# Rebuilding 32-bit weights from 64-bit words: a scaled copy on ScalarE in place of a mask, and three VectorE instructions per piece in another order

## The chip, the cores and the metric

The kernel runs on one core of a Trainium2 chip. The metric is the device time of one execution in microseconds (us), as the median of several runs. The engines of the core work from queues of their own, each strictly in order: PE (TensorE) multiplies matrices, DVE (VectorE) and ACT (ScalarE) do elementwise work, POOL (GpSimd) has only a little to do at the start, and SP (SyncE) issues most of the DMAs. An instruction waits for others through semaphores; whatever stands behind a waiting instruction in its queue waits too.

## The reference

```python
def _attn_ref(x, w_r, w_i, b_r, b_i):            # x: (2, 3008, 256)
    X = np.fft.rfft(x, axis=1)
    Yr = Xr @ w_r - Xi @ w_i + b_r
    Yi = Xr @ w_i + Xi @ w_r + b_i
    Yr = np.sign(Yr) * np.maximum(np.abs(Yr) - 0.01, 0.0)   # Yi the same
    return np.fft.irfft(Yr + 1j * Yi, n=3008, axis=1)

def _moe_ref(x, w_in, w_out):                     # d_ff 2048, on 6016 tokens
    h = x @ w_in
    return (h * np.clip(h + 3.0, 0.0, 6.0) / 6.0) @ w_out

def _moe2_ref(x, w_gate, w_val, w_out):           # d_ff 1536
    g = x @ w_gate
    return ((g / (1.0 + np.exp(-g))) * (x @ w_val)) @ w_out
```

The five weight matrices of the two dense layers come as 64-bit floats; everything is computed in 32 bits.

## The kernel before, in words

**Stages.** A Fourier stage comes first: `pre` (first transform, L242 on PE, with copies `bs` on ACT at L245 and DVE at L247), `s2` (second transform, L284, whose result is split into a high part `xh` by ACT at L288 and L289 and a low part `xl` by DVE at L118), `ln` (24 small products, L113 to L115 with tile `p`, then `yb`, `yc`, `yp` on DVE at L319 to L323), `ia` and `post` (back transforms, L330 and L416). Each product is three matmuls, low times high, high times low and high times high, so every operand needs both parts. The first dense layer follows as 192 *units* of a block of up to 512 tokens and one of 16 column groups (`project1`, tile `ph`; `lower`, tiles `gh` and `gl`; `outp`, tile `acc`), and begins while the second half of the Fourier stage still runs. The second dense layer comes last (`quad`, from L652 on).

**Order.** Nothing is reordered: each queue has its instructions in the order in which the program writes them. The list `seq` sets it for the Fourier stage: for each step, `ln` half 0, `ia`, a `pre`, the two halves of `s2` for the next step, `ln` half 1, a `pre` while there are any, `ia`. Within `s2` the second half's `xh` stands on ACT behind a negated copy (L291) of the first half's `xl`, so DVE and ACT take turns there.

**The weights.** The class `Convert` turns the 64-bit weights into 32-bit ones, piece by piece (128 partitions of 256 numbers): 32 pieces for the first dense layer (`conv1`) and 36 for the second (`conv2`). A DMA on SP brings a piece into tile `st` (four buffers). Of each number the upper word H has the sign, 11 bits of exponent and 20 of mantissa, the lower word L the other 32. A 32-bit float is put together from them by shifts and masks on DVE, in tile `wt`: L164 takes H three bits to the left and masks it, L165 puts the top three bits of L below, L166 the two top bits of H above, and L172 multiplies by zero where the number is too small, by comparing a mask `mask` that ACT made by squaring H (L156). Each of L165, L166 and L172 reads what the instruction just ahead of it wrote. For `conv1`, ACT then makes the high part (L175, `w1h`) two steps later, and DVE the low part (L179, `w1l`) three steps later. `step` runs the stages of different pieces one after the other. Its calls stand at fixed places: in `ln`, in the later `pre` and, twice at most, in each of the first units, so `conv1` is done shortly after the Fourier stage. `conv2` runs beside the units, one step for two units, and its results go back to HBM (`Wd`), to be fetched for the second dense layer.

Of the kernel before, what the change touches and what calls it, by code (L numbers as in the profile page):

```python
# [9 lines left out]
F32 = mybir.dt.float32  # L10
F32R = mybir.dt.float32r
I64 = mybir.dt.int64
U32 = mybir.dt.uint32
AF = mybir.ActivationFunctionType
ALU = mybir.AluOpType
# [10 lines left out]
NQ = NG // 4  # L26
LAM = 0.01

LEAST = 1.125 * 2.0**-15
FF1, FF2 = 2048, 1536  # L30
KF1, KF2 = FF1 // 128, FF2 // 128
BLK = 512
# [45 lines left out]
def fourier_moe_kernel(ctx: ExitStack, tc: tile.TileContext, x, lin, bias, w1, w2, fwd1, inv2, fwd2,  # L78
                       inv1, out):
    nc = tc.nc  # L80

    def pool(stack, name, side):
        return stack.enter_context(tc.tile_pool(name=name, bufs=1, side=side))
# [33 lines left out]
    def low(o, full, hi):  # L117
        nc.vector.tensor_tensor(out=o, in0=full, in1=hi.bitcast(F32), op=ALU.subtract)  # L118
# [11 lines left out]
    wst = pool(ctx, "wst", "left")  # L130
# [6 lines left out]
    class Convert:  # L137
# [2 lines left out]

        def __init__(self, pieces):
            self.pieces = pieces
            self.st, self.mask, self.full = {}, {}, {}
            self.at = -3

        def done(self):
# [4 lines left out]
            nc.sync.dma_start(t, self.pieces[i][0])  # L151
            self.st[i] = t.bitcast(U32).rearrange("p (n t) -> p n t", t=2)

        def square(self, i):
            m = wst.tile([128, 256], F32, tag="mask", name="mask", bufs=2)
            nc.scalar.activation(m, self.st[i][:, :, 1].bitcast(F32), AF.Square)  # L156
            self.mask[i] = m

        def words(self, i, to=None):
            st, m = self.st.pop(i), self.mask.pop(i)  # L160
            H, L = st[:, :, 1], st[:, :, 0]
            t = wst.tile([128, 256], U32, tag="wt", name="wt", bufs=4)
            v = nc.vector
            v.tensor_scalar(t, H, 3, 0x3FFFFFF8, op0=ALU.logical_shift_left, op1=ALU.bitwise_and)  # L164
            v.scalar_tensor_tensor(out=t, in0=L, scalar=29, in1=t, op0=ALU.logical_shift_right, op1=ALU.bitwise_or)  # L165
            v.scalar_tensor_tensor(out=t, in0=H, scalar=0xC0000000, in1=t, op0=ALU.bitwise_and, op1=ALU.bitwise_or)  # L166
            tf = t.bitcast(F32)
            if to is None:
                to = self.full[i] = tf
            else:  # L170
                m, tf = (a.rearrange("p (a b) -> p a b", b=128) for a in (m, tf))
            v.scalar_tensor_tensor(out=to, in0=m, scalar=LEAST * LEAST, in1=tf, op0=ALU.is_ge, op1=ALU.mult)  # L172

        def high(self, i):
            nc.scalar.copy(self.pieces[i][1], self.full[i])  # L175
# [5 lines left out]
        def step(self):  # L181
            i = self.at
            self.at += 1
            for at, stage in ((i - 3, self.low), (i - 2, self.high), (i + 1, self.square), (i, self.words), (i + 3, self.load)):
                if 0 <= at < len(self.pieces):
                    stage(at)

# [32 lines left out]
    p = psf[0]([128, 512], "p0")  # L220
# [130 lines left out]
    def L(p):  # L351
        return [lambda h=h: ln(*ORDER[p], h) for h in range(2)]

    def A(p):
        return [lambda h=h: ia(*ORDER[p], h) for h in range(2)] if p >= 0 else [lambda: None] * 2
# [9 lines left out]
    for p in range(len(ORDER)):  # L365
        l, a = L(p), A(p - 1)
# [101 lines left out]
    for k, after in zip(blocks, blocks[1:]):  # L468
        for f, step in ((2, lambda k=after: load_ct(k)), (7, lambda k=after: post(k, 0)),
                        (9, lambda k=after: post(k, 1))):  # L470
            extra.setdefault((k, f), []).append(step)

    at = [0]
    more = []

    def unit():

        n = at[0]
        at[0] += 1

        for _ in range(2):
            if conv1.at < 2 * n + 6 and not conv1.done():
                conv1.step()
        if 0 <= n - 1 < len(units):
            lower(units[n - 1])
        if n < len(units):
            k, f = units[n]
            state[units[n]] = project1(k, f, ntok(k))
        if n >= 2:
            outp(units[n - 2])  # L490
        if n < len(units):
            for step in extra.get(units[n], ()):
                step()
        for f in more:
            f(n)
# [16 lines left out]
    def ring():  # L512
        return cv.tile([128, SLOT, 128], F32R, tag="slot", name="slot", bufs=4)

    class Convert2(Convert):
# [8 lines left out]
            return full[f, 2]  # L524

        def steps(self):
            for i in range(3):
                self.load(i)
            self.square(0)
            yield  # L530
            for f in range(KF2):
                for what in range(3):
                    i = 3 * f + what
                    if i + 3 < len(self.pieces):
                        self.load(i + 3)
                    if i + 1 < len(self.pieces):
                        self.square(i + 1)
                    self.words(i, self.full_of(i))
                    yield
                F = full.pop(f)  # L540
                for o, x, y, op in ((4, 0, 3, ALU.add), (5, 4, 1, ALU.subtract), (6, 1, 0, ALU.subtract), (7, 2, 5, ALU.subtract)):
                    nc.vector.tensor_tensor(out=F[:, o], in0=F[:, x], in1=F[:, y], op=op)
                t = ring()
                nc.scalar.copy(t[:, :7], F[:, 1:])
                yield
                O = full.pop((f, 2))
                nc.scalar.copy(t[:, 14:16], O)
                low(t[:, 7:14], F[:, 1:], t[:, :7])
                yield
                low(t[:, 16:], O, t[:, 14:16])  # L550
                nc.sync.dma_start(Wd[f], t.bitcast(F32).rearrange("p a b -> p (a b)"))
                yield
# [59 lines left out]
    def beside(n):  # L612
        if not conv1.done():
            conv1.step()
        elif n % 2 == 0:
            next(steps, None)
        left = len(units) + 2 - n
        if left <= 28:
            next(first, lambda: None)()
        if left in (8, 4):  # L620
            fetch(2 - left // 4)

    more.append(beside)
    while at[0] < len(units) + 2:
        unit()
    assert next(steps, True) and next(first, None) is None


# [170 lines left out]
```

## Time and profile before

| | us |
|---|---|
| median of 3 runs | 1257.1 |
| lowest, highest | 1257.02, 1259.64 |
| span of the profiled execution, first to last instruction | 1255.8 |
| PE busy | 1233.0 |
| DVE busy | 845.7 |
| ACT busy | 679.5 |

The profile is of one execution. A busy time is the time in which an engine's instructions ran; a PE that is busy may still run at half its clock, so the granted clock has to be read with it. What an engine waits for is given as the releaser, the instruction whose semaphore came last. Of each instruction the timeline has the start and the duration; on DVE and ACT an instruction can start a little before the end of the one ahead.

### The profile page before, as it was taken

The numbers are of one execution on the slowest core, as the hardware profiler recorded it, in microseconds if no ns is written. First come the engines' busy times: TensorE is split into PE (matmuls) and PEld (weight loads), VectorE is DVE, ScalarE is ACT, GpSimd is POOL, SyncE is SP. The second block draws the span as 40 slices with busy tenths as digits, with TensorE's granted clock in tenths as the row PEclk, the third lists the DMA queues.
The fourth block names the chain that finished last, engine by engine and source line by source line (L and its number), as shares of the span: only waits on it lengthen the run. The fifth ranks groups of instructions, "written<-read, shape, count | busy, mean of one in ns | idle before, by whom it ended". The sixth has DMA issues, their size and how long they took to land.

```text
span 1255.8 us, 15966 instructions
## 1 busy us (share of the span) xinstructions
PE 1233.0 (98%) x5914; PEld 1035.6 (82%) x5914; DVE 845.7 (67%) x1492; ACT 679.5 (54%) x1216; POOL 6.3 (0%) x15
## 2 busy tenths in 40 slices
PE   8889999999999999999999999999999999999998
PEld 2789898788888888888889878888888888888997
DVE  2588767676666676676666567677676676666665
ACT  2344445455555555555555465566556665555554
POOL 1000000000000000000000000000000000000000
PEclk9899999999999999999999999999999999999999
DMA  9965511231321221232132054554544644544551
GB/s 300 277 220 160 169 42 64 93 99 63 97 95 55 90 89 49 93 99 83 54 104 91 25 212 151 201 187 169 203 166 156 229 171 153 214 153 164 207 184 72
DMA packets 50286, 172.85 MB, mean 138 GB/s; under 512 B 4752, under 2 KB 18160, under 8 KB 39456
## 3 DMA queue, kind: packets, MB, share of 16 engines
q1 hardware_dynamic: 41856, 158.55, 36.7%
q10 hardware_dynamic: 8128, 12.58, 2.9%
q8 instruction: 46, 0.75, 0.2%
q0 software_dynamic: 224, 0.69, 0.2%
q14 instruction: 32, 0.26, 0.1%
HBM read 132.75 MB, written 39.06 MB: 137 GB/s over the span
## 4 chain that ended last, share of the span: by engine, by line
PE 90%; DVE 5%; DMA 2%; ACT 2%; issue 1%; ACTq 0%; DVEq 0%; SPq 0%
PE acc L114 12%; PE acc L115 12%; PE acc L113 12%; PE ph L113 7%; PE ph L115 7%; PE ph L114 7%; PE P L652 5%; PE P L654 5%; PE P L653 5%; PE p L416 3%; PE Tb L652 3%; PE Tb L653 3%; PE Tb L654 3%; PE Q L652 1%; PE Q L654 1%; PE Q L653 1%
## 5 line engine op out<-in xcount | busy, mean ns | idle before, releaser
L118 DVE TENSOR_TENSOR gl<-r,gh 128x512 fp32r<-128x512 f32 (+1 forms) x192 | 130.1, 677 | 79.8 <-ACT gh L449 78.6
L430 ACT ACTIVATE r<-ph,three 128x512 f32<-128x512 f32 (+1 forms) x192 | 130.2, 678 | 96.5 <-PE ph L115 78.3
L431 DVE SCALAR_TENSOR_TENSOR r<-r,ph 128x512 f32<-128x512 f32 (+1 forms) x192 | 129.4, 674 | 61.1 <-ACT r L430 60.4
L449 ACT CAST gh<-r 128x512 fp32r<-128x512 f32 (+1 forms) x192 | 117.4, 611 | 87.5 <-DVE r L431 86.6
L113 PE MATMUL ph<-xah,w1l 128*128 128x512 f32 (+1 forms) x384 | 152.2, 396 | 0.7 <-DVE w1l L179 0.7
L113 PE MATMUL acc<-gh,w1l 128*128 128x512 f32 (+1 forms) x384 | 148.3, 386 | 1.0 <-ACT gh L449 1.0
L114 PE MATMUL acc<-gl,w1h 128*128 128x512 f32 (+1 forms) x384 | 148.3, 386 | 0.6 <-DVE gl L118 0.5
L115 PE MATMUL ph<-xah,w1h 128*128 128x512 f32 (+1 forms) x384 | 148.2, 386 | 0.0
L114 PE MATMUL ph<-xal,w1h 128*128 128x512 f32 (+1 forms) x384 | 148.2, 386 | 0.0
L115 PE MATMUL acc<-gh,w1h 128*128 128x512 f32 (+1 forms) x384 | 148.1, 386 | 0.0
L118 DVE TENSOR_TENSOR gl<-s,gh 128x512 fp32r<-128x512 f32 (+1 forms) x144 | 97.2, 675 | 49.5 <-ACT gh L676 49.5
L652 PE MATMUL P<-xo,slot 128*128 128x512 f32 (+1 forms) x288 | 111.3, 386 | 1.7 <-DVE g L722 0.8
L114 PE MATMUL acc<-gl,slot 128*128 128x512 f32 (+1 forms) x288 | 111.1, 386 | 0.3 <-DVE gl L118 0.2
L113 PE MATMUL acc<-gh,slot 128*128 128x512 f32 (+1 forms) x288 | 111.0, 385 | 0.0
L654 PE MATMUL P<-xo,slot 128*128 128x512 f32 (+1 forms) x288 | 110.9, 385 | 0.0
L653 PE MATMUL P<-xo,slot 128*128 128x512 f32 (+1 forms) x288 | 110.9, 385 | 0.0
L115 PE MATMUL acc<-gh,slot 128*128 128x512 f32 (+1 forms) x288 | 110.9, 385 | 0.0
L718 ACT ACTIVATE s<-g 128x512 f32<-128x512 f32 (+1 forms) x72 | 44.9, 623 | 93.2 <-DVE g L716 93.2
L676 ACT CAST gh<-s 128x512 fp32r<-128x512 f32 (+1 forms) x144 | 88.1, 612 | 1.8 <-DVE s L735 1.6
L114 PEld LDWEIGHTS acc<-gl,w1h 128*128 128x128 f32 x384 | 72.1, 188 | 15.3 <-DVE gl L118 1.7
L113 PEld LDWEIGHTS acc<-gh,w1l 128*128 128x128 f32 x384 | 72.1, 188 | 15.1 <-ACT gh L449 1.5
L113 PEld LDWEIGHTS ph<-xah,w1l 128*128 128x128 f32 x384 | 72.2, 188 | 14.2 <-issue 0.8
(95 smaller groups left out, 2292.9 us busy)
## 6 DMA issues: line engine op xcount, KB each, us to landing
slot<-Wd SPq DMA_DIRECT2D x72, 1152.0 KB, 5.0
st<-in_w SPq DMA_DIRECT2D x68, 256.0 KB, 3.2
Wd<-slot SPq DMA_DIRECT2D x12, 1152.0 KB, 4.7
x<-in_x SPq DMA_DIRECT2D x16, 384.0 KB, 6.2
Bd<-bs ACTq DMA_DIRECT2D x16, 384.0 KB, 5.1
z<-Bd SPq DMA_DIRECT2D x12, 512.0 KB, 5.5
Cd<-cs ACTq DMA_DIRECT2D x12, 512.0 KB, 3.3
Xd<-x SPq DMA_DIRECT2D x20, 256.0 KB, 2.1
```

Of the source, the lines that this page charges most:

```text
L113: nc.tensor.matmul(o, wl, xh, start=start, stop=False)
L114: nc.tensor.matmul(o, wh, xl, start=False, stop=False)
L115: nc.tensor.matmul(o, wh, xh, start=False, stop=stop)
L118: nc.vector.tensor_tensor(out=o, in0=full, in1=hi.bitcast(F32), op=ALU.subtract)
L430: nc.scalar.activation(r[:, :n], p[:, :n], AF.Relu, bias=three)
L431: nc.vector.scalar_tensor_tensor(out=r[:, :n], in0=r[:, :n], scalar=6.0, in1=p[:, :n], op0=ALU.min, op1=ALU.mult)
L449: nc.scalar.copy(hi[:, :n], g[:, :n])
L652: nc.tensor.matmul(o, wl, x[:, 0, :n], start=start, stop=False, skip_group_check=not start)
L653: nc.tensor.matmul(o, wh, x[:, 1, :n], start=False, stop=False, skip_group_check=not start)
L654: nc.tensor.matmul(o, wh, x[:, 0, :n], start=False, stop=True, skip_group_check=not start)
L676: nc.scalar.copy(hi[:, :nb], t[:, :nb])
L718: nc.scalar.activation(s0[:, :n], h, AF.Silu)
```

## The change

ACT no longer squares H. It copies it, read as a 32-bit float and multiplied by 2**-112 (`scale`, tile `head`, three buffers). Read so, H has the upper eight of the eleven exponent bits as its exponent, and the factor subtracts 112 from them: that is the difference of the two formats' exponent offsets, and numbers that are too small become zero by it. DVE then has three instructions per piece where it had four: `shift` (L161 of the new file) takes `head` three bits to the left, `tail` (L165) puts in the top bits of L, and `sign` (L174) the sign bit of `head`. In a step they are those of two pieces: `shift` of piece i, `sign` of piece i - 1, `tail` of piece i. `sign`, the last of a piece, is thus a step later than L172 was; `high` and `low` keep their steps. In `conv2` the load of a piece and the ACT copy are issued behind the DVE instructions of a step instead of ahead of them, and there is one step more.

```diff
+HEAD = 2.0**-112
...
-        def square(self, i):
-            m = wst.tile([128, 256], F32, tag="mask", name="mask", bufs=2)
-            nc.scalar.activation(m, self.st[i][:, :, 1].bitcast(F32), AF.Square)
-            self.mask[i] = m
-
-        def words(self, i, to=None):
-            st, m = self.st.pop(i), self.mask.pop(i)
-            H, L = st[:, :, 1], st[:, :, 0]
-            t = wst.tile([128, 256], U32, tag="wt", name="wt", bufs=4)
-            v = nc.vector
-            v.tensor_scalar(t, H, 3, 0x3FFFFFF8, op0=ALU.logical_shift_left, op1=ALU.bitwise_and)
-            v.scalar_tensor_tensor(out=t, in0=L, scalar=29, in1=t, op0=ALU.logical_shift_right, op1=ALU.bitwise_or)
-            v.scalar_tensor_tensor(out=t, in0=H, scalar=0xC0000000, in1=t, op0=ALU.bitwise_and, op1=ALU.bitwise_or)
-            tf = t.bitcast(F32)
...
-            v.scalar_tensor_tensor(out=to, in0=m, scalar=LEAST * LEAST, in1=tf, op0=ALU.is_ge, op1=ALU.mult)
+        def scale(self, i):
+            m = wst.tile([128, 256], F32, tag="head", name="head", bufs=3)
+            nc.scalar.mul(m, self.st[i][:, :, 1].bitcast(F32), HEAD)
+            self.head[i] = m.bitcast(U32)
+
+        def shift(self, i):
+            self.word[i] = wst.tile([128, 256], U32, tag="wt", name="wt", bufs=4)
+            nc.vector.tensor_scalar(self.word[i], self.head[i], 3, None, op0=ALU.logical_shift_left)
+
+        def tail(self, i):
+            t, L = self.word[i], self.st.pop(i)[:, :, 0]
+            nc.vector.scalar_tensor_tensor(out=t, in0=L, scalar=29, in1=t, op0=ALU.logical_shift_right, op1=ALU.bitwise_or)
+
+        def sign(self, i, to=None):
+            h, t = self.head.pop(i), self.word.pop(i)
...
+            nc.vector.scalar_tensor_tensor(out=to, in0=h, scalar=0x80000000, in1=t, op0=ALU.bitwise_and, op1=ALU.bitwise_or)
...
-            for at, stage in ((i - 3, self.low), (i - 2, self.high), (i + 1, self.square), (i, self.words), (i + 3, self.load)):
+            for at, stage in ((i - 3, self.low), (i - 2, self.high), (i, self.shift), (i - 1, self.sign), (i, self.tail),
+                              (i + 1, self.scale), (i + 3, self.load)):
...
-            for f in range(KF2):
-                for what in range(3):
-                    i = 3 * f + what
-                    if i + 3 < len(self.pieces):
-                        self.load(i + 3)
-                    if i + 1 < len(self.pieces):
-                        self.square(i + 1)
-                    self.words(i, self.full_of(i))
-                    yield
+            for i in range(n + 1):
+                if i < n:
+                    self.shift(i)
+                if i > 0:
+                    self.sign(i - 1, self.full_of(i - 1))
+                if i < n:
+                    self.tail(i)
+                if i + 3 < n:
+                    self.load(i + 3)
+                if i + 1 < n:
+                    self.scale(i + 1)
+                yield
+                f, what = divmod(i - 1, 3)
+                if f < 0 or what < 2:
+                    continue
```

DVE's queue in the Fourier stage, from the last `bs` copy to the two low parts `xl` of the fourth `s2` step, before (a name in brackets is an engine's semaphore or that of a DMA queue):

```order
L247 COPY bs_7_650<-p_1_7_1_654 96x512 [waits DMAHW2_49,PE_49]
L179 TENSOR_TENSOR w1l_123<-wt,w1h_122 128x256 [waits Activation_49]
L164 TENSOR_SCALAR wt<-st 128x256 [waits DMAHW0_49]
L165 SCALAR_TENSOR_TENSOR wt<-st,wt 128x256 [waits DVE_49]
L166 SCALAR_TENSOR_TENSOR wt<-st,wt 128x256 [waits DVE_49]
L172 SCALAR_TENSOR_TENSOR wt<-mask,wt 128x256 [waits DVE_49,Activation_49]
L118 TENSOR_TENSOR xl_3_675<-p_0_3_0_676,xh_3_674 128x4x128 [waits PE_49,Activation_49]
L118 TENSOR_TENSOR xl_3_675<-p_0_3_1_685,xh_3_674 128x4x128 [waits PE_49,Activation_49]
```

The same place of DVE's queue now (all lines behind the new code are two or three higher):

```order
L250 COPY bs_7_641<-p_1_7_1_645 96x512 [waits DMAHW2_49,PE_49]
L181 TENSOR_TENSOR w1l_123<-wt,w1h_122 128x256 [waits Activation_49]
L161 TENSOR_SCALAR wt<-head 128x256 [waits Activation_49]
L174 SCALAR_TENSOR_TENSOR wt<-head,wt 128x256
L165 SCALAR_TENSOR_TENSOR wt<-st,wt 128x256 [waits DMAHW0_49,DVE_49]
L118 TENSOR_TENSOR xl_3_665<-p_0_3_0_666,xh_3_664 128x4x128 [waits PE_49,Activation_49]
L118 TENSOR_TENSOR xl_3_665<-p_0_3_1_675,xh_3_664 128x4x128 [waits PE_49,Activation_49]
```

One instruction is gone, and the wait for ACT has moved from the last instruction of a piece to its first, L161; of the other two, L174 works on the piece before.

ACT's queue where two steps of `conv1` stand in one unit, near the end of the Fourier stage, before:

```order
L175 CAST w1h_142<-wt 128x256
L156 ACTIVATE mask<-st 128x256 [waits DMAHW6_49]
L175 CAST w1h_142<-wt 128x256
L156 ACTIVATE mask<-st 128x256 [waits DMAHW0_49,DVE_49]
L449 CAST gh<-r 128x512
L430 ACTIVATE r<-ph,three 128x512 [waits PE_49]
```

ACT's queue at that place now:

```order
L177 CAST w1h_142<-wt 128x256
L156 ACTIVATE head<-st 128x256 [waits DMAHW6_49]
L177 CAST w1h_142<-wt 128x256 [waits DVE_49]
L156 ACTIVATE head<-st 128x256 [waits DMAHW0_49]
L452 CAST gh<-r 128x512
L433 ACTIVATE r<-ph,three 128x512 [waits PE_49]
```

The instructions are as many and stand in the same order; the wait for DVE went from the second L156 (for a buffer of `mask`) to the high part just ahead of it (for the `sign` of its piece).

## Rows read from the trace of the kernel before

**Rows 1.** The page's first part: busy us, share of the span, instructions of each engine

```profile
PE 1233.0 (98%) x5914; PEld 1035.6 (82%) x5914; DVE 845.7 (67%) x1492; ACT 679.5 (54%) x1216; POOL 6.3 (0%) x15
```

**Rows 2.** Stretches: length, busy PE, PEld, DVE, ACT, POOL; granted clock; DMA share; GB/s

```profile
38.40:74.28 35.88, 35.00 (x228) 29.10 (x228) 28.09 (x62) 15.67 (x39) 0.00 (x0) 1.00 0.83 261
...
79.28:82.80 3.52, 3.52 (x17) 3.52 (x18) 3.35 (x8) 2.25 (x6) 0.00 (x0) 0.52 0.40 88
...
92.46:101.81 9.35, 9.35 (x74) 9.10 (x73) 7.73 (x18) 4.71 (x12) 0.00 (x0) 1.00 0.56 192
...
111.81:121.82 10.01, 9.62 (x74) 9.16 (x73) 8.36 (x19) 4.93 (x13) 0.00 (x0) 1.00 0.49 160
121.82:128.66 6.84, 6.40 (x50) 5.86 (x48) 5.32 (x12) 2.81 (x7) 0.00 (x0) 1.00 0.79 225
184.00:209.56 25.56, 24.59 (x137) 20.73 (x135) 24.15 (x56) 12.62 (x28) 0.00 (x0) 1.00 0.17 52
...
250.00:700.00 450.00, 450.00 (x2126) 381.83 (x2125) 303.70 (x558) 244.36 (x409) 0.00 (x0) 1.00 0.24 81
```

**Rows 3.** PE's waits from 40 to 212 us: in total, times, longest

```profile
PE p L113 <- DVE xl L118: 5.2, 5, 2.7
```

**Rows 4.** PE's timeline, 60 to 80 us: start, duration, instruction, count, idle before and releaser

```profile
66.38 1.03 PE L330 MATMUL p<-yp,n 128*128 128x256 f32 x4
67.25 1.88 PE L242 MATMUL p<-x,fwd_sb 96*96 96x512 f32 x4
...
71.11 0.28 PE L113 MATMUL p<-linh,xl 128*128 128x256 f32 x1
...
71.47 0.28 PE L113 MATMUL p<-linh,xl 128*128 128x256 f32 x1
...
73.63 1.03 PE L330 MATMUL p<-yp,n 128*128 128x256 f32 x4
...
77.35 0.39 PE L113 MATMUL p<-linh,xl 128*128 128x256 f32 x1 [2.69 <-DVE xl L118]
...
79.28 0.51 PE L113 MATMUL p<-linh,xl 128*128 128x256 f32 x1 [0.86 <-DVE xl L118]
```

**Rows 5.** PE's timeline, 198 to 210 us: first and last of three waits

```profile
199.24 0.47 PE L113 MATMUL ph<-xah,w1l 128*128 128x512 f32 x1 [0.41 <-DVE w1l L179]
...
209.56 0.50 PE L113 MATMUL ph<-xah,w1l 128*128 128x512 f32 x1 [0.26 <-DVE w1l L179]
```

**Rows 6.** DVE's timeline, 70 to 77 us: one piece, and what follows up to `xl`

```profile
70.51 0.28 DVE L164 TENSOR_SCALAR wt<-st 128x256 uint32<-128x256 uint32 x1
70.83 0.43 DVE L165 SCALAR_TENSOR_TENSOR wt<-st,wt 128x256 uint32<-128x256 uint32 x1
71.29 0.42 DVE L166 SCALAR_TENSOR_TENSOR wt<-st,wt 128x256 uint32<-128x256 uint32 x1
71.82 0.42 DVE L172 SCALAR_TENSOR_TENSOR wt<-mask,wt 128x256 f32<-128x256 f32 x1
72.16 0.68 DVE L319 TENSOR_TENSOR yb<-p,bias_sb 128x512 f32<-128x512 f32 x1
...
73.95 0.68 DVE L247 COPY bs<-p 96x512 f32<-96x512 f32 x1
...
76.60 0.69 DVE L118 TENSOR_TENSOR xl<-p,xh 128x512 fp32r<-128x512 f32 x1
```

**Rows 7.** ACT's timeline, 74 to 77 us, between that `bs` and that `xl`

```profile
74.72 0.31 ACTq L249 DMA_DIRECT2D Bd<-bs  x1
...
75.38 0.43 ACT L156 ACTIVATE mask<-st 128x256 f32<-128x256 f32 x1
```

**Rows 8.** The instructions on tile `wt`: duration min/median/max in ns, first and last start

```profile
L172 DVE SCALAR_TENSOR_TENSOR wo<-mask,wt x12: 425/426/427, 243.7 to 627.6; 128x256 f32<-128x256 f32 x12
```

**Rows 9.** ACT's timeline: the first piece of `conv2`

```profile
226.74 0.43 ACT L156 ACTIVATE mask<-st 128x256 f32<-128x256 f32 x1 [4.46 <-DMA st<-in_w]
```

**Rows 10.** ACT's waits from 180 to 215 us: in total, times, longest

```profile
ACT cs L331 <- PE p L330: 3.6, 3, 1.8
```

More of the change, by code (lines that the diff above doesn't have):

```diff
@@ L27 @@
 LAM = 0.01
-LEAST = 1.125 * 2.0**-15
+HEAD = 2.0**-112
 FF1, FF2 = 2048, 1536
@@ L142, in __init__ @@
             self.pieces = pieces
-            self.st, self.mask, self.full = {}, {}, {}
+            self.st, self.head, self.word, self.full = {}, {}, {}, {}
             self.at = -3
@@ L152, in load @@
             self.st[i] = t.bitcast(U32).rearrange("p (n t) -> p n t", t=2)
-        def square(self, i):
-            m = wst.tile([128, 256], F32, tag="mask", name="mask", bufs=2)
-            nc.scalar.activation(m, self.st[i][:, :, 1].bitcast(F32), AF.Square)
-            self.mask[i] = m
-        def words(self, i, to=None):
-            st, m = self.st.pop(i), self.mask.pop(i)
-            H, L = st[:, :, 1], st[:, :, 0]
-            t = wst.tile([128, 256], U32, tag="wt", name="wt", bufs=4)
-            v = nc.vector
-            v.tensor_scalar(t, H, 3, 0x3FFFFFF8, op0=ALU.logical_shift_left, op1=ALU.bitwise_and)
-            v.scalar_tensor_tensor(out=t, in0=L, scalar=29, in1=t, op0=ALU.logical_shift_right, op1=ALU.bitwise_or)
-            v.scalar_tensor_tensor(out=t, in0=H, scalar=0xC0000000, in1=t, op0=ALU.bitwise_and, op1=ALU.bitwise_or)
-            tf = t.bitcast(F32)
+        def scale(self, i):
[10 more added lines that the diff above has]
+            h, t = self.head.pop(i), self.word.pop(i)
             if to is None:
-                to = self.full[i] = tf
+                to, self.full[i] = t, t.bitcast(F32)
             else:
-                m, tf = (a.rearrange("p (a b) -> p a b", b=128) for a in (m, tf))
-            v.scalar_tensor_tensor(out=to, in0=m, scalar=LEAST * LEAST, in1=tf, op0=ALU.is_ge, op1=ALU.mult)
+                h, t = (a.rearrange("p (a b) -> p a b", b=128) for a in (h, t))
+                to = to.bitcast(U32)
+            nc.vector.scalar_tensor_tensor(out=to, in0=h, scalar=0x80000000, in1=t, op0=ALU.bitwise_and, op1=ALU.bitwise_or)
         def high(self, i):
@@ L526, in steps @@
         def steps(self):
+            n = len(self.pieces)
             for i in range(3):
                 self.load(i)
-            self.square(0)
+            self.scale(0)
             yield
-            for f in range(KF2):
-                for what in range(3):
-                    i = 3 * f + what
-                    if i + 3 < len(self.pieces):
-                        self.load(i + 3)
-                    if i + 1 < len(self.pieces):
-                        self.square(i + 1)
-                    self.words(i, self.full_of(i))
-                    yield
+            for i in range(n + 1):
[13 more added lines that the diff above has]
+                    continue
                 F = full.pop(f)
```

## The prediction, made before the changed kernel ran

> **What bounds the kernel now.** Start with the page's first part: PE is busy for 98% of the span [rows 1]. That alone would say that nothing on VectorE (DVE) matters. A mean hides stages, so the next view is a table of stretches. From 250 to 700 us, where the 36 pieces of `conv2` are converted, PE is busy for 450.00 of 450.00 us at full clock, with DVE at 303.70 [rows 2]. There DVE has room, and what it is spared is worth nothing. In the Fourier stage it is otherwise. Between 184 and 209.56 us DVE is busy for 24.15 of 25.56 us, and PE falls short by about 1 us; a period of the stage, cut at the same `ia` matmuls, takes 9.35 us when PE never waits, but 10.01 us from 111.81 on, with 0.39 us of PE idle [rows 2]. The view of waits says on whom: PE waits 5.2 us for DVE's `xl` between 40 and 212 us, the longest time 2.7 us [rows 3]. So three places on PE end with DVE, and only there can the change be worth anything.
>
> *Place A, 74 to 83 us.* The `ia` group at 66.38 is followed by the next matmul at 67.25, so after the one at 73.63 the next was due at 74.50; it came at 77.35, 2.85 us late [rows 4]. Six matmuls later PE waits again, 0.86 us idle before 79.28, the second half of the same `xl` [rows 4]. An idle time is counted from the end of the matmul ahead, 0.16 us after the next could have begun (1.03 against 0.87 us in that group), so about 1.0 us is lost here. Behind these waits the granted clock is 0.52 for 3.52 us: 17 matmuls [rows 2] that at full clock take 0.12 us each (0.36 us for three, 71.11 to 71.47 [rows 4]), or 2.0 us, so 1.5 us is lost while the clock is at 1.2 instead of 2.4 GHz. Together 2.85 + 1.0 + 1.5 = 5.35 us.
>
> *Place B, 102 to 129 us.* Two periods like the one from 111.81, each 0.66 us longer than 9.35, and 0.44 us of idle in the last part (0.6 with the same 0.16) [rows 2]: 1.9 us.
>
> *Place C, 198 to 210 us.* Three waits of 0.26 to 0.41 us for `w1l` and `gl` [rows 5], 1.0 us in all, with 0.16 each 1.5 us.
>
> **The change, step by step.** *DVE.* A piece now takes 72.16 - 70.51 = 1.65 us of DVE's queue [rows 6]: 0.32 from L164 to L165, 0.46 to L166, 0.53 to L172, which waits on two semaphores, and 0.34 to `yb`, which needs nothing of it and starts 0.08 us before L172 ends. Where each instruction reads what the one ahead wrote, the next starts 0.03 us after its end or later; where not, 0.08 us before it. The new group has an instruction less, and between `shift` and `tail` of a piece stands `sign` of another. I take `shift` as L164 (0.28 us) and the other two as L172 (0.42): 0.20 + 0.34 + 0.34 = 0.88 us. Bounds: no form like `shift`, one operation on a packed tile, is in the trace; it lies between L164 and L165, 0.28 to 0.43 us, and I take the lower since it is the same operation on the same size. `tail` waits on two semaphores as L172 does; that cost L172 0.07 us, and costs 0 to 0.07 here, 0 taken, because both were signalled before `sign` ends. If the order bought nothing, the group would take 0.31 + 0.46 + 0.46 = 1.23 us. So a piece spares 0.42 to 0.77 us; I take 0.7, a little under the top, since not every L172 has the double wait.
>
> *ACT.* A copy with a factor in place of a square: same engine, form and size, so 0.43 us [rows 7] either way. The wait of L156 for a `mask` buffer becomes the wait of the high part just ahead for `sign`, the same step of DVE, and one instruction earlier in it: nothing. *SP.* In `conv2` the load moves behind the DVE and ACT work of its step, but nothing else is issued between, and the buffer it waits for is freed by the same step: nothing. *One step more* in `conv2`: its last piece is done by 628 us [rows 8], the second layer begins after 700: nothing, covered by some 70 us. *The first piece of `conv2`* is scaled right behind its own load, as it was squared before; ACT waits 4.46 us for the DMA there [rows 9], `gh` stands behind it, and that stays.
>
> *A after the change.* DVE has eight pieces in its queue between 42 us and the `bs` at 73.95, and hardly idles there (28.09 busy of 35.88 us, the rest being turns with ACT [rows 2]). Eight times 0.7 is 5.6 us, but `bs` reads what L242 made, which ends at 67.25 + 1.88 = 69.13 [rows 4]: so it moves by 4.8 us at most. From `bs` to `xl` the path goes through ACT (issue at 74.72, the mask at 75.38, `xh`, then `xl` at 76.60 [rows 6, 7]) and keeps its length. So `xl` is 4.8 us earlier. Needed are 2.85 us for the first half and, the second half being due 0.91 us after the first at 75.4 where it came at 79.28, 3.9 us for the second. Both waits go, with 0.9 us to spare, and the half clock behind them. Next late is PE itself. *B:* two pieces per period, 1.4 us off a loop of 10.01: DVE would need 8.6, PE 9.35. All 1.9 us go. *C:* four pieces stand in DVE's queue from 184 us to the first of these waits, 2.8 us against 0.57. All 1.5 us go.
>
> The sum: 5.35 + 1.9 + 1.5 = 8.75 us from the span of 1255.8 us, 1247.05. PE's work behind these places is without a wait for DVE to 700 us, so nothing gives it back. The median of the runs lies 1.3 us above the profiled span, so **1248.3 us**.
>
> **A rule against it.** The trace has an independent DVE instruction start 0.08 us ahead of the other's end, and a dependent one at least 0.03 after [rows 6]. The Trainium skill, "VectorE: DVE Perf Modes", section "Rules for kernel authors", says of chained DVE instructions that the drain of the pipe comes regardless, and that one should lessen their count and not the semaphores; by it the order buys nothing and the group takes 1.23 us, which [rows 6] speak against.
>
> **Rivals.** *1. Only the count helps.* A piece spares 0.42 us: eight make 3.4 us at `bs`, enough for the first half of `xl`, 0.5 us short for the second. PE then idles about as long as in B, where the clock stayed at 1.00 [rows 2]. B: 0.84 against 0.66, still gone; C: 1.7 against 0.57, gone. 1248.3 + 0.5 = 1248.8; with half a clock loss as well, up to 1250. For it: a `shift` nearer to 0.43 us. Against it: the 0.34 us ahead of `yb` [rows 6]. The rule above would give this time.
>
> *2. ScalarE holds `shift`: slower.* ACT's result is now needed by the first of the three, and behind it in DVE's queue stand `yb`, `yp`, `bs` and `xl`, for which PE waits. If each piece is held as long as ACT itself is held by PE at most near place C, 1.8 us [rows 10], it costs 1.8 - 0.7 = 1.1 us more than now. That is 8 pieces before A, some 10 in B's periods and 6 in C, 26 us: 1283. It decides from 0.7 us per piece on. Against it: the copy is issued a step ahead; the square for the next piece ran at 75.38, before even `xl` at 76.60, and that piece comes behind both halves of `xl` [rows 6, 7].
>
> *3. The DMA engines become late.* Their share from 38 to 74 us is 0.83 [rows 2], 29.8 us of work; with 4.8 us less time it is 0.96. A late table or `z` would give PE a wait of some 2 us and a half clock of 1.5: 1251.8. Against it: what the next step needs is issued a period ahead, and a weight two steps ahead.
>
> *4. Nothing moves.* What `xl` waits for beside DVE is as late, ACT above all: 1257.1. Against it: ACT is busy for 15.67 of 35.88 us [rows 2].
>
> **How the numbers follow.** The forecast has 0.74 (1247 to 1249.5 by itself), rival 1 0.12, rival 3 0.04, rival 4 0.06, rival 2 0.04. The range 1246 to 1251.5 holds the forecast and rival 1. The low end is the forecast with some of the 0.1 to 0.2 us that the first matmul behind each wait takes longer; the high end takes in rival 1 with its clock and most of rival 3. A measurement of this kernel can tell about 0.2%, 2.5 us. Faster by more: 0.74 + 0.12 + 0.04 = 0.90; within: 0.06; slower: 0.04.
>
> **What would show it.** In the changed profile, per piece, `shift`, `sign` and `tail` should take some 0.9 us from the first start to the next instruction's, and `tail` should start before `sign` ends. PE should have no wait for `xl` after 45 us, the granted clock should be 1.00 from 40 us on, all periods should be near 9.35 us, and the wait for the first load of `conv2` should still be there, some 9 us earlier. A group of 1.2 us would speak for rival 1; DVE idle before `shift`, released by ACT, for rival 2; waits of PE or ACT for a DMA between 60 and 100 us for rival 3. The prediction is wrong if PE is no longer full between 250 and 700 us, or if the clock falls elsewhere.

## The result, and the profile after

| | before | after |
|---|---|---|
| median, us (beside each other on one chip) | 1258.05 | 1247.29 |
| lowest to highest | 1257.02 to 1259.64 | 1246.49 to 1249.81 |
| span of the profiled execution | 1255.8 | 1245.9 |

The ratio is 0.9919, with a 95% interval of 0.9906 to 0.9932: faster, by 10.8 us if the two medians are subtracted and by some 10 by the ratio. The forecast was 1248.3 in a range of 1246.0 to 1251.5.

The first part of the page and the chain of work by engine, after:

```profile
PE 1228.3 (99%) x5914; PEld 1034.2 (83%) x5914; DVE 809.8 (65%) x1424; ACT 679.7 (55%) x1216; POOL 6.3 (1%) x15
...
PE 96%; DMA 2%; DVE 0%; ACT 0%; issue 0%; SPq 0%; ACTq 0%; DVEq 0%
```

The same two lines before were [rows 1] and this chain:

```profile
PE 90%; DVE 5%; DMA 2%; ACT 2%; issue 1%; ACTq 0%; DVEq 0%; SPq 0%
```

DVE has 68 instructions and 35.9 us of work less, yet the time fell by some 10 us. What changed for PE is that DVE's 5% of the chain went to zero (the share itself is no price: 5% of the span are some 63 us, most of which PE's own work takes now). PE's waits over the whole span of after (in total, times, longest) show what is left:

```profile
PE p L287 <- DMA z<-Bd: 6.4, 1, 6.4
PE p L245 <- DMA x<-in_x: 1.6, 3, 0.7
PE p L225 <- DVE zeros L127: 1.5, 1, 1.5
PE acc L113 <- ACT gh L452: 1.5, 1, 1.5
...
PE acc L114 <- DVE gl L118: 0.4, 2, 0.2
PE p L113 <- DVE xl L118: 0.3, 1, 0.3
```

Of the 5.2 us for `xl` in [rows 3] one wait of 0.3 us is left, at 40 us, and `w1l` [rows 5] is gone from the list. Stretches of after (columns as in [rows 2]): up to place A, the part with places A and B, one period cut at the `ia` matmuls, the part with place C, and the full part:

```profile
39.70:73.31 33.61, 33.28 (x219) 27.65 (x219) 25.06 (x58) 17.74 (x43) 0.00 (x0) 1.00 0.91 283
73.31:120.51 47.20, 47.20 (x367) 46.01 (x365) 37.66 (x85) 25.88 (x64) 0.00 (x0) 1.00 0.66 213
...
104.85:114.12 9.27, 9.27 (x75) 9.05 (x74) 7.23 (x18) 5.03 (x12) 0.00 (x0) 1.00 0.55 188
...
174.60:199.46 24.86, 24.86 (x148) 22.10 (x146) 22.34 (x52) 13.21 (x30) 0.00 (x0) 1.00 0.18 54
...
250.00:700.00 450.00, 450.00 (x2130) 382.59 (x2129) 286.92 (x523) 242.65 (x407) 0.00 (x0) 1.00 0.24 80
```

and the same 367 matmuls of A and B before:

```profile
73.63:128.66 55.03, 50.24 (x367) 47.64 (x365) 45.34 (x99) 27.18 (x67) 0.00 (x0) 0.97 0.61 192
```

PE is busy for all of the 47.20 us, at a granted clock of 1.00, where it took 55.03 us. From 250 to 700 us PE was full before [rows 2] and is full now, with 16.8 us less work on DVE: nothing gained there.

DVE's timeline of after: one piece, then `bs`, then the two halves of `xl` at place A:

```profile
64.43 0.28 DVE L161 TENSOR_SCALAR wt<-head 128x256 uint32<-128x256 uint32 x1
64.63 0.41 DVE L174 SCALAR_TENSOR_TENSOR wt<-head,wt 128x256 uint32<-128x256 uint32 x1
64.97 0.42 DVE L165 SCALAR_TENSOR_TENSOR wt<-st,wt 128x256 uint32<-128x256 uint32 x1
65.30 0.41 DVE L181 TENSOR_TENSOR w1l<-wt,w1h 128x256 fp32r<-128x256 f32 x1
...
68.85 0.69 DVE L250 COPY bs<-p 96x512 f32<-96x512 f32 x1 [0.47 <-PE p L245]
...
71.52 0.69 DVE L118 TENSOR_TENSOR xl<-p,xh 128x512 fp32r<-128x512 f32 x1 [0.78 <-ACT xh L292]
73.45 0.69 DVE L118 TENSOR_TENSOR xl<-p,xh 128x512 fp32r<-128x512 f32 x1 [1.24 <-ACT xh L292]
```

and PE's timeline behind it, where [rows 4] had idle times of 2.69 and 0.86 us:

```profile
66.93 1.88 PE L245 MATMUL p<-x,fwd_sb 96*96 96x512 f32 x4
...
73.31 1.03 PE L333 MATMUL p<-yp,n 128*128 128x256 f32 x4
...
73.99 0.47 PE L113 MATMUL p<-linh,xl 128*128 128x256 f32 x1
...
74.89 0.28 PE L113 MATMUL p<-linh,xl 128*128 128x256 f32 x1
```

A piece takes 65.30 - 64.43 = 0.87 us, and L165 starts at 64.97, before L174 ends at 65.04. `bs` now waits 0.47 us for PE: DVE has caught up with PE, and being faster still could not move it. The first matmul on `xl` (73.99) follows `ia` without a wait, and the second half of `xl`, done at 73.45 + 0.69 = 74.14, is there 0.75 us before its matmul at 74.89.

**Where the 9.9 us of span went**, from one matmul to the same one in both traces: 0.32 up to the `ia` at 73.63 or 73.31; 55.03 - 47.20 = 7.83 in A and B; 1.95 in C (from 128.66 to 209.56 before, 80.90 us; from 120.51 to 199.46 after, 78.95 us); some 0.2 given back behind it. The 7.83 are 5.66 up to the matmul at 82.79 before and 76.81 after (5.98 - 0.32), where the half clock of before is over, and 2.17 for the rest.

### The profile page after: what moved, and what is told of

It reads as the page before. It is cut to its first block, busy times and chain, and to the rows that moved or that the text cites. A ratio compares the mean times of both kernels' runs of the same rounds, so it can differ in the third digit from the quotient of the medians.

```text
span 1245.9 us, 15942 instructions
## 1 busy us (share of the span) xinstructions
PE 1228.3 (99%) x5914; PEld 1034.2 (83%) x5914; DVE 809.8 (65%) x1424; ACT 679.7 (55%) x1216; POOL 6.3 (1%) x15
## 4 chain that ended last, share of the span: by engine, by line
PE 96%; DMA 2%; DVE 0%; ACT 0%; issue 0%; SPq 0%; ACTq 0%; DVEq 0%
PE acc L114 12%; PE acc L115 12%; PE acc L113 12%; PE ph L113 7%; PE ph L115 7%; PE ph L114 7%; PE P L662 5%; PE P L663 5%; PE P L664 5%; PE Tb L663 3%; PE Tb L662 3%; PE Tb L664 3%; PE p L419 3%; PE p L113 2%; PE p L115 2%; PE p L114 2%
## 5 line engine op out<-in xcount | busy, mean ns | idle before, releaser
L115 PEld LDWEIGHTS ph<-xah,w1h 128*128 128x128 f32 x384 | 72.1, 188 | 14.0
```

The costliest lines, as they stand in the source:

```text
L115: nc.tensor.matmul(o, wh, xh, start=False, stop=stop)
```

## Experiments

The theory: three places of the Fourier stage end with DVE, and a shorter group per piece takes DVE off PE's path there; all else is hidden. Rivals: the saved instruction does it and the order nothing (or the other way round); `conv2` has a share; the third buffer on ACT, or the copy that ACT now makes in place of a square, does it. The length of the group is read from the start of `shift` to the start of the next instruction that is not of the piece.

**The count alone: `e1_count`.** Three instructions, but those of one piece, each needing the one ahead.

```diff
-(i, self.shift), (i - 1, self.sign), (i, self.tail),
+(i, self.shift), (i, self.tail), (i, self.sign),
```

> In the first layer's weights shift, tail and sign of one piece follow each other, so each again needs the one just ahead; the second layer's are as in the changed kernel. Theory (the length of a piece's group in VectorE's queue decides): the group takes about 1.2 us from shift to the next instruction (0.32 + 0.07 for a double wait + 0.46 + 0.34), which spares 0.4 us of 1.6; eight pieces make 3.4 us where 2.85 and 3.9 are needed, so PE waits 0.3 to 0.5 us once for xl near 74 us at full clock, all periods are near 9.35 us: 1247.5 to 1249. Rival 'only the order': as before, 1257 to 1258. Rival 'only the count': as the changed kernel, 1247.3.

Measured: 1248.3 us (1246.91 to 1249.52), ratio 0.9927 (0.9911 to 0.9943). A piece on DVE, and the two halves of `xl` at A:

```profile
66.54 0.28 DVE L161 TENSOR_SCALAR wt<-head 128x256 uint32<-128x256 uint32 x1
66.86 0.43 DVE L165 SCALAR_TENSOR_TENSOR wt<-st,wt 128x256 uint32<-128x256 uint32 x1
67.32 0.42 DVE L174 SCALAR_TENSOR_TENSOR wt<-head,wt 128x256 uint32<-128x256 uint32 x1
67.67 0.68 DVE L322 TENSOR_TENSOR yb<-p,bias_sb 128x512 f32<-128x512 f32 x1
...
72.10 0.69 DVE L118 TENSOR_TENSOR xl<-p,xh 128x512 fp32r<-128x512 f32 x1 [0.51 <-ACT xh L292]
74.03 0.69 DVE L118 TENSOR_TENSOR xl<-p,xh 128x512 fp32r<-128x512 f32 x1 [1.24 <-ACT xh L292]
```

and PE's matmul on the second half:

```profile
74.78 0.39 PE L113 MATMUL p<-linh,xl 128*128 128x256 f32 x1
```

The group is 1.13 us, not 0.87: the order does save 0.26 us of queue. But `xl` starts only 0.58 us later than after, and PE shows no wait at A, where 0.3 to 0.5 us were expected: the second half is done at 74.72, just in time. Up to 218 us the two kernels are level. What the profiled execution is longer by (a span of 1247.5 in place of 1245.9 us) sits elsewhere: at the first load of `conv2` PE waits 1.34 us (1.47 after), and behind that wait the clock is at half in e1_count,

```profile
218.06 0.50 PE L113 MATMUL acc<-gh,w1l 128*128 128x512 f32 x1 [1.34 <-ACT gh L452]
```

```profile
219.62:223.03 3.41, 3.41 (x10) 2.63 (x9) 2.61 (x5) 1.90 (x4) 0.00 (x0) 0.50 0.05 8
```

which it is not after. From 219.59 to 223.23 e1_count needs 3.64 us for what takes 2.04 us after (219.64 to 221.68): 1.60 us (the last experiment returns to this).

**The order alone: `e2_order`.** The four instructions of before and the square on ACT, interleaved over two pieces, with a third `mask` buffer, for `conv1`.

```diff
-((i - 3, self.low), (i - 2, self.high), (i + 1, self.square), (i, self.words), (i + 3, self.load))
+((i - 3, self.low), (i - 2, self.high), (i + 1, self.square), (i, self.w0), (i - 1, self.w2),
+ (i, self.w1), (i - 1, self.w3), (i + 3, self.load))
```

`w0` to `w3` are L164, L165, L166 and L172 of before, one each.

> The kernel before with its four instructions and its square, but in the first layer's weights those of two pieces in turn, so that none needs the one just ahead (three mask buffers for it). Theory (length of the group): 0.20 + 3 x 0.34 = 1.22 us per piece, the same length as with one instruction less in the old order: 1247.5 to 1249. Rival 'only the count': 1257 to 1258, as before. Rival 'only the order': 1247.3.

Measured: 1248.76 us (1247.92 to 1250.08), ratio 0.9932 (0.9917 to 0.9947). One step's instructions on DVE:

```profile
67.14 0.28 DVE L177 TENSOR_SCALAR wt<-st 128x256 uint32<-128x256 uint32 x1
67.34 0.41 DVE L185 SCALAR_TENSOR_TENSOR wt<-st,wt 128x256 uint32<-128x256 uint32 x1
67.68 0.41 DVE L181 SCALAR_TENSOR_TENSOR wt<-st,wt 128x256 uint32<-128x256 uint32 x1
68.01 0.42 DVE L190 SCALAR_TENSOR_TENSOR wt<-mask,wt 128x256 f32<-128x256 f32 x1
68.35 0.68 DVE L338 TENSOR_TENSOR yb<-p,bias_sb 128x512 f32<-128x512 f32 x1
```

and PE at A:

```profile
75.45 0.39 PE L113 MATMUL p<-linh,xl 128*128 128x256 f32 x1 [0.54 <-DVE xl L118]
```

The same four instructions that took 1.65 us [rows 6] take 1.21 us, and 2.69 us of waiting become 0.54. (It also has a wait of 1.0 us for the DMA of `ct` at 122.42, at the matmul where the kernel before waited 0.44 us and the changed kernel does not.) Count and order are each enough by themselves for nearly all of the gain.

**How much is spare: `e5_one_more` and `e6_two_more`.** The changed kernel with one further DVE instruction of L174's kind and size per piece of `conv1` (on a tile of zeros, 0.34 us of queue), and with two. Nothing is left out of the computation; what the added instruction writes is never used.

```diff
+        def more(self, i):
+            nc.vector.scalar_tensor_tensor(out=zeros[:, :256], in0=zeros[:, 256:], scalar=1.0, in1=zeros[:, 256:], op0=ALU.mult, op1=ALU.add)
...
-(i, self.shift), (i - 1, self.sign), (i, self.tail),
+(i, self.shift), (i - 1, self.sign), (i, self.tail), (i, self.more),
```

In `e6_two_more` a second `(i, self.more)` stands behind `low`, so a piece's group begins with it there.

> The changed kernel with one more VectorE instruction per piece in the first layer's weights (128 x 256, needs nothing, its result is not used). Theory: the group is 0.34 us longer, 1.22 us: again the same length, 1247.5 to 1249, PE waits for xl at most 0.5 us near 74 us. Rival 'some other part of the change than the length of the queue (the wait for ScalarE, the buffers)': as the changed kernel, 1247.3, with no wait at all.

> The changed kernel with two more such instructions per piece. Theory: the group is 1.56 us, what it was before (1.58 to 1.65): the waits for xl near 74 us, the half clock behind them, the 10.0 us periods and the waits for w1l near 200 us are back, 1255 to 1258. Rival 'some other part of the change': 1247.3 to 1249.

Measured: 1248.46 us (1247.33 to 1249.4), ratio 0.9927 (0.991 to 0.9944) with one; 1255.24 us (1254.29 to 1257.22), ratio 0.9981 (0.9971 to 0.9991) with two. The first instruction of a piece's group on DVE and the first behind the group, with one added and then with two:

```profile
67.96 0.28 DVE L161 TENSOR_SCALAR wt<-head 128x256 uint32<-128x256 uint32 x1
...
69.17 0.68 DVE L325 TENSOR_TENSOR yb<-p,bias_sb 128x512 f32<-128x512 f32 x1
```

```profile
67.40 0.41 DVE L177 SCALAR_TENSOR_TENSOR zeros<-zeros 128x256 f32<-128x256 f32 x1
...
68.94 0.41 DVE L184 TENSOR_TENSOR w1l<-wt,w1h 128x256 fp32r<-128x256 f32 x1
```

PE at A with one, and then with two:

```profile
76.29 0.38 PE L113 MATMUL p<-linh,xl 128*128 128x256 f32 x1 [0.55 <-DVE xl L118]
```

```profile
75.99 0.44 PE L113 MATMUL p<-linh,xl 128*128 128x256 f32 x1 [1.85 <-DVE xl L118]
...
77.92 0.58 PE L113 MATMUL p<-linh,xl 128*128 128x256 f32 x1 [0.43 <-DVE xl L118]
```

With two, also the stretch behind the first wait and a period of B:

```profile
76.18:79.59 3.41, 2.98 (x14) 2.69 (x14) 2.41 (x7) 2.50 (x7) 0.00 (x0) 0.50 0.66 234
...
99.99:109.85 9.86, 9.61 (x74) 9.15 (x73) 8.48 (x21) 4.91 (x14) 0.00 (x0) 1.00 0.55 160
```

The picture of before is back, nearly at its full size: both waits at A, a half clock that begins behind the first of them, a period of 9.86 us in B, and the waits for `w1l` near 200 us (0.6 us). Put side by side:

| kernel | DVE per piece, us | PE idle at A, us | clock behind it | median, us |
|---|---|---|---|---|
| after | 0.87 | 0 | 1.00 | 1247.29 |
| e1_count | 1.13 | 0 | 1.00 | 1248.3 |
| e2_order | 1.21 | 0.54 | 1.00 | 1248.76 |
| e5_one_more | 1.21 | 0.55 | 1.00 | 1248.46 |
| e6_two_more | 1.54 | 1.85 + 0.43 | 0.50 | 1255.24 |
| before | 1.65 | 2.69 + 0.86 | 0.52 | 1257.1 to 1258.1 |

This is no straight line. From 0.87 to 1.21 us the time hardly moves (the intervals of the four ratios overlap), from 1.21 to 1.54 it moves by 6.8 us. The first part of the gain is large because a wait, the clock behind it and the periods of B go together; the last 0.3 us per piece is nearly all slack. What ACT makes, a square or a scaled copy, does not matter: e2_order has the square and nearly the whole gain, e6_two_more the copy and a fifth of it.

**Which layer: `e3_first_layer` and `e4_second_layer`.** The change for `conv1` alone (with `conv2` converted as before, by `square` and `words`), and for `conv2` alone; both with three buffers on ACT's side.

```diff
 e3_first_layer, against after, in Convert2.steps:
-            self.scale(0)
+            self.square(0)
...
+                    self.words(i, self.full_of(i))
```

> The change for the first layer's 32 pieces alone; the second layer's 36 are converted as before (with three mask buffers). Theory (only the Fourier stage is limited by VectorE): the whole gain, 1246.5 to 1248.5. Rival 'every piece counts': 36 of 68 pieces are without it, 1252 to 1253.

> The change for the second layer's 36 pieces alone; the first layer's are converted as before. Theory: nothing, 1256.5 to 1258.5, PE full from 250 to 700 us as before. Rival 'every piece counts': 1252 to 1253.

Measured: 1246.92 us (1246.3 to 1251.72), ratio 0.9924 (0.9903 to 0.9945) for `conv1` alone; 1257.59 us (1256.29 to 1259.12), ratio 1.0001 (0.9992 to 1.0011) for `conv2` alone. In e3_first_layer DVE keeps the old work of `conv2`, and PE is full all the same:

```profile
250.00:690.00 440.00, 440.00 (x2082) 373.59 (x2082) 297.12 (x546) 238.26 (x399) 0.00 (x0) 1.00 0.25 83
```

while e4_second_layer keeps the waits for `xl` (45 to 212 us):

```profile
PE p L114 <- DVE xl L119: 4.3, 4, 2.7
```

All of the gain comes from the 32 pieces of `conv1`.

**The third buffer: `e8_three_masks`.** Before, with three `mask` buffers in place of two.

```diff
-            m = wst.tile([128, 256], F32, tag="mask", name="mask", bufs=2)
+            m = wst.tile([128, 256], F32, tag="mask", name="mask", bufs=3)
```

> The kernel before with three mask buffers in place of two, as the changed kernel has three of head; ScalarE's waits for a mask buffer (7.4 us in all) go. Theory: VectorE's queue is as long as before, nothing, 1256.5 to 1258.5. Rival 'ScalarE's waits for a buffer held up xh': most of the gain, 1247 to 1251.

Measured: 1258.32 us (1256.83 to 1259.63), ratio 1.0006 (0.9997 to 1.0016). ACT's waits for a `mask` buffer (7.4 us before) are gone, but PE's wait for `xl` (45 to 212 us) is what it was:

```profile
PE p L113 <- DVE xl L118: 4.4, 4, 2.7
```

The buffer is worth nothing, so e2_order's gain is the order's.

**The wait that stayed: `e7_later_scale` and `e10_before_later`.** ACT's first copy of `conv2` stands right behind its own load, and `gh` behind it. Here it comes one step later, in the changed kernel and (with `square`) in the one before.

```diff
             for i in range(3):
                 self.load(i)
+            yield
             self.scale(0)
             yield
```

> The changed kernel, with the first scaled copy of the second layer's weights one step (two units, 5.4 us) behind its load, not right behind it. Theory: ScalarE no longer waits 4.9 us for that DMA with gh behind it; PE's wait of 1.5 us for gh near 218 us goes, with the slow start behind it: 2.0 to 2.3 us less than the changed kernel, 1245. Rival 'PE waits there for something else too (the block's end, ct)': less than 1 us, 1246.5 to 1247.3.

> The kernel before with one added yield: ScalarE's first square of conv2 is issued one step behind the three loads. The gain of e7_later_scale over the changed kernel is theory: it takes away PE's wait for the first load of conv2 (1.05 us and 0.23 us in the kernel before, with the first matmul behind it slower) and nothing of the Fourier stage. Expected: 1.3 to 1.8 us below the kernel before, 1255.5 to 1256, ratio 0.9987, PE's wait for xl as before (5.2 us). Rival: the 1.8 us came from the new conversion being free earlier, and the kernel before keeps its time: ratio 1.000.

Measured: 1245.48 us (1244.8 to 1245.76), ratio 0.9903 (0.9889 to 0.9918), the lowest median so far; and 1255.39 us (1254.7 to 1256.86), ratio 0.9983 (0.9974 to 0.9992). ACT at that piece, in after and then in e7_later_scale:

```profile
217.12 0.43 ACT L156 ACTIVATE head<-st 128x256 f32<-128x256 f32 x1 [4.88 <-DMA st<-in_w]
```

```profile
217.30 0.42 ACT L156 ACTIVATE head<-st 128x256 f32<-128x256 f32 x1
```

The wait is gone, and with it, by the medians, 1.8 us in the changed kernel, somewhat less than the 2.0 to 2.3 expected. These two were not run beside each other, and the intervals of their ratios overlap; the kernel before was, and its interval lies below 1. There 2.3 us go, somewhat more than the 1.3 to 1.8 expected, with the waits for `xl` left (40 to 240 us):

```profile
PE p L113 <- DVE xl L118: 4.0, 4, 2.7
```

So this gain belongs to neither way of converting.

**Where e1_count's microsecond was: `e9_count_later`.** e1_count with the same added `yield`.

```diff
                 self.load(i)
+            yield
             self.scale(0)
```

> e1_count with the first ScalarE copy of conv2 issued one step behind the three loads, as in e7_later_scale. e1_count had the same wait of 1.34 us for conv2's first load as the changed kernel (1.47 us), but behind it 3.4 us at half clock, some 1.3 us lost, which the changed kernel did not have. If that half clock is all that e1_count lies behind the changed kernel, taking the wait away gives both the wait (about 1.8 us, as e7_later_scale gained on the changed kernel) and the clock back: 1248.3 - 1.8 - 1.3 = 1245.2 to 1245.6, the same as e7_later_scale, with no stretch at half clock behind 40 us. If the order of the three costs something by itself in the Fourier stage, this kernel stays about 1 us behind e7_later_scale: 1246.5.

Measured: 1245.43 us (1244.77 to 1246.35), ratio 0.9901 (0.9886 to 0.9916), against 1245.48 for e7_later_scale. From 40 to 240 us:

```profile
40.00:240.00 200.00, 199.31 (x1258) 178.22 (x1259) 146.71 (x297) 103.82 (x226) 0.00 (x0) 1.00 0.48 149
```

The clock is 1.00 throughout and PE idles for 0.7 us, at 40 us. With that wait out of both, the order of the three instructions makes no difference to the time that these runs can tell. With the wait in, the microsecond between the medians is one of single executions: two of e1_count's four took 1246.91 and 1247.33 us, two 1249.28 (the profiled one, with the half clock) and 1249.52, and one of the changed kernel's four took 1249.81. With the wait out, all eight lie between 1244.77 and 1246.35. The mean granted clock of the two other long ones is 0.994 and of the short ones 0.997, so their clock fell more too; that it fell at this place is not shown, for one execution of each kernel has a profile.

## Why the prediction was right, and where not

- **Place A and place B**, 5.35 + 1.9 = 7.25 us: measured 7.83 together. `xl` was to come at 71.8 and came at 71.52, capped where the prediction had the cap, by the end of L245 (66.93 + 1.88 = 68.81, `bs` at 68.85). All waits went, and the half clock. Some terms were a little small: the matmul behind `ia` was due 0.68 us after it (73.31 to 73.99) and not 0.87; a period without a wait is 9.27 us and not 9.35; and the first matmul behind a wait, 0.1 to 0.2 us longer than the others, was left out of the sum. One wait was put down to the wrong engine: the last 0.44 us of B are by the view of waits (before, 40 to 212 us) ACT's and not DVE's:

```profile
PE p L416 <- ACT xh L289: 0.4, 1, 0.4
```

  It went all the same; by which step is not shown.
- **Place C**, 1.5 us: measured 1.95, with PE busy for 24.86 of 24.86 us.
- **The sum**, 8.75 us: measured 9.9 of span, 1.1 more than forecast. The median lies 1.4 us above the span (the prediction took 1.3), so the time came out at 1247.29, 1.0 below the forecast. That it is so near is in part luck: the executions of the changed kernel spread over 3.3 us, and the median of before that the prediction started from, 1257.1, is 1258.05 with one execution more.
- **The group of a piece**, 0.88 us: 0.87. `shift` takes 286 ns in the median, the lower of its two bounds; the two semaphores of `tail` cost nothing, also taken right.
- **Nothing for `conv2`, SP and the further step**: right (e4_second_layer: 1.0001). **Nothing for ACT's form**: right (e2_order and e6_two_more).
- **The first load of `conv2`** was to stay, and stayed, but with 1.47 us for PE where it was 1.05. The copy on ACT waits 4.88 us, where it was 4.46 [rows 9]: the place comes 9.6 us earlier, and the median of all loads of weights went from 3.2 to 3.8 us from issue to landing; whether the one caused the other is not shown. So 0.4 us was given back there, which makes the 0.2 net behind place C.
- **Rival 3**, the DMAs: the share up to place A did rise, from 0.83 to 0.91, and `z` takes 6.1 us in place of 5.5 from issue to landing. No wait of PE or ACT came of it between 60 and 100 us. The direction was right, and it was hidden.
- **Rival 2**, ScalarE holding `shift`: no idle time of DVE before L161 shows in the Fourier stage.
- **Rival 1**, only the count helps, has to be split. That the order buys nothing is wrong: four instructions in another order took 1.21 us in place of 1.65 and made the kernel 0.0068 faster in ratio (e2_order). The rule of the Trainium skill, "VectorE: DVE Perf Modes", section "Rules for kernel authors", to lessen the count and not the semaphores since the drain comes regardless, does not hold here in so far as it gives the order nothing; that is what this number shows. That a lower count helps does hold (e1_count). But that the count alone would leave some 0.5 us of PE idle at A was wrong as well. The group is 1.13 us (e1_count), not 1.23: the prediction gave its last instruction 0.46 us, where [rows 6] has 0.34 from L172 to `yb`, and 0.35 was measured. So a piece spares 0.52 us and not 0.42, eight make 4.2 us, over the 3.9 needed, and PE shows no wait. The two halves of the change do not add up: either gives nearly everything.

The step of the argument that carried the forecast, then, was to set what `xl` gains against what PE needs at A, 2.85 us for its first half and 3.9 for its second; what goes beyond that counts for nothing. Eight times what a piece spares against before foretells A in every kernel of the table: 4.2 us in e1_count, just enough; 3.5 us in e2_order and e5_one_more, 0.4 short for the second half, where PE idles 0.54 and 0.55 us; 0.9 us in e6_two_more, short for both. The cap on `bs`, 4.8 in place of 5.6 us, set the time of `xl` but not the sum, since both are more than 3.9; to spare were 0.75 us where the prediction had 0.9.

Open stays what the last 0.3 us per piece are worth where DVE is nearer to its limit; this kernel has no such place any more.

## What to carry to other kernels

Look for the stretch in which the engine ends a wait of the bounding one, and work out how far that wait can move before something else is late; a saving beyond that is slack, and two edits that each come near it do not add up. Where a chain of dependent VectorE instructions stands on such a path, interleaving two chains was here about as good as taking one instruction of four out (1.21 and 1.13 us per piece), and cost a buffer. An instruction on an in-order queue that stands right behind its own load makes all that follow wait for the DMA: here one step of distance gave 1.8 us.

## What the runs showed of the hardware

- Where an instruction on DVE does not need the one ahead, it starts 0.07 to 0.08 us before that one's end (64.97 against 65.04, in after); where it does, 0.03 to 0.04 us after (66.86 against 66.82 and 67.32 against 67.29, in e1_count). Between them is some 0.11 us for each instruction of 128x256; four in a row with a double wait differ by 0.44 us (1.65 and 1.21).
- The clock behind a wait is no fixed price. After 1.47 + 0.22 us of idle PE the granted clock stayed at 1.00, in this row of after,

```profile
219.00:222.00 3.00, 3.00 (x14) 2.48 (x15) 2.28 (x5) 2.14 (x5) 0.00 (x0) 1.00 0.03 5
```

  and after 1.34 + 0.23 us at the same place in e1_count it was at 0.50 for 3.41 us. So a wait of this length is to be priced with a half clock as a possibility, 1.6 us in e1_count, and not as a certainty; why it fell in the one and not in the other no run here tells.
